# An attention kernel whose first batch scores both heads of a pair in turn, and whose batch-closing pairs spread their reciprocals by TensorE

## The chip, the cores and the metric

One Trainium2 chip, one of its cores. The metric is device time of the whole program in microseconds (us). Of the kernel before there are three runs with a median of 806.53 us (805.07 to 807.45).

## What is computed

Block-causal attention over 4 batches, 8 heads, 576 positions and a head size of 64, then a gated spatial unit, then a two-layer MLP with a residual. Cut to what matters here:

```python
scores = q @ k.T / sqrt(64)                 # per batch and head, 576 x 576
scores = where(row // 64 >= col // 64, scores, -1e9)
attn = exp(scores - max(scores))
attn = attn / (sum(attn) + 1e-9)
x = attn @ v                                # heads side by side: 576 x 512 per batch
h = relu(x @ w_in); u, v2 = split(h)        # 1024 columns
v_s = w_spatial @ layernorm(v2) + b_spatial
y = (u * v_s) @ w_out
out = y + relu(layernorm(y) * g @ w_ch1) @ w_ch2
```

## The kernel before

Attention goes by pairs of heads, four pairs to a batch, 16 in all. A pair is nine units (`UNITS`, line 231): first the last 64 rows of both heads together (chunk 4, two PSUM banks of 256 and 320 columns), then the chunks 3, 2, 1 and 0 of 128 rows, each for head 0 and then for head 1. The loop at line 533 runs over all units `u`. `scores(u)` (line 238) multiplies q and k into PSUM; `softmax(u)` (line 287) lets VectorE (DVE) mask the scores and take the minimum into an SBUF tile and ScalarE (ACT) take the exponential, with its sum into a column of `sm`; `transposes(u - 2)` (line 338) turns the result by TensorE into a PSUM bank, from which DVE or ACT copies it; `weighted` (line 389) multiplies it with v, in two parts (`pH` at the pair's unit 7, `pL` at unit 2 of the next pair), and ACT copies that out into `xx`.

The first `PACKED` = 4 pairs, which are batch 0, keep one head in the partitions 0 to 63 and the other in 64 to 127: a score product has 64 contraction rows, and a unit three products of split fp32 (high times high, high times low, low times high) into one bank. The first three units are plain fp32. From pair 4 on the splits are stacked to 128 rows and a unit has two products (line 281).

`reciprocals(p)` (line 310), at the first unit of the next pair, inverts the pair's row sums (128 partitions x 9 columns), transposes them, lets ACT copy them out, and spreads them over 64 partitions a head by a trip through DRAM: two stores, two loads that broadcast. `store_x(p)` (line 411), at unit 5 of the next pair, multiplies `xx` with them and splits the product into two fp32r parts in `xT`: three operations on GpSimd (POOL).

When a batch's four pairs are in `xT`, its products with `w_in` follow (`w_in_stage`, line 495: value tiles `vps`, then gate tiles `ups`). They are a generator from which `fill` (line 506) takes some products at each unit of the next batch, from the unit `dstart` = 8 of that batch on; the last batch's run after the loop. The weights `w_in` are unpacked (`decode`, line 81: ACT, then two operations on DVE, then two on POOL) at the units of the list `DECODE` (line 532), for the first time at unit 1.

PSUM has eight banks: three for matmul results (`p_mm`), three for scores (`p_sc`), two for transpositions (`p_tr`). Each engine works through its own queue in order. The order in the queues comes from the program's order and from a planner that simulates the program and moves ready instructions ahead. SP's queue issues all DMAs.

Of the kernel before, what the change touches and what calls it, by code (L numbers as in the profile page):

```python
# [8 lines left out]
F32 = mybir.dt.float32  # L9
# [4 lines left out]
ALU = mybir.AluOpType  # L14
AX = mybir.AxisListType
PSUM = bass.MemoryType.PSUM
# [17 lines left out]
def tile_kernel(  # L34
# [26 lines left out]
    NB, NP, _, _, _, S = qk.shape  # L61
# [7 lines left out]
    NPAIR = NB * NP  # L69
    MM = nc.tensor.matmul  # L70
# [66 lines left out]
    PACKED = PLAN['packed']  # L137
# [43 lines left out]
    idle = p_mm.tile([128, 512], F32, tag="mm", name="idle")  # L181

    def warm(n):
        for _ in range(n):
# [11 lines left out]
    ops = {}  # L196
# [35 lines left out]
    NU = len(UNITS)  # L232
    PLAIN = PLAN['plain']
    state = {}

    sums = {}

    def scores(u):
        p = u // NU
        j, c = UNITS[u % NU]  # L240
        st, qt, _, raw = ops[p]
        banks = []
        plain = u < PLAIN
        if c == 4:
            sums[p] = at.tile([128, 9], F32, tag="sm", name="sm")
            for a, z in ((0, 256), (256, S)):
                s_ps = p_sc.tile([128, 512], F32, tag="sc", name="sc")
                for h in range(2) if plain else ():
                    rows = slice(64 * h, 64 * h + 64)
                    MM(  # L250
                        s_ps[rows, :z - a], lhsT=raw[rows, 0, 0, 512:S], rhs=raw[rows, 0, 1, a:z],
                        start=True, stop=True,
                    )
                if not plain and p < PACKED:
                    for n, (x, y) in enumerate(((0, 0), (0, 1), (1, 0))):
                        MM(s_ps[:, :z - a], lhsT=qt[:, x, 0, :], rhs=st[:, y, 1, a:z], start=(n == 0), stop=(n == 2))
                elif not plain:
                    for h in range(2):
                        for i in range(2):
                            MM(  # L260
                                s_ps[:, :z - a], lhsT=qt[:, i, h, :], rhs=st[:, h, 2, a:z],
                                start=(h == 0 and i == 0), stop=(h == 1 and i == 1),
                            )
                banks.append((s_ps, a, z - a))
        else:
            n = 128 * (c + 1)
            nn = max(n, 192)
            q = slice(128 * c, 128 * c + 128)
            s_ps = p_sc.tile([128, 512], F32, tag="sc", name="sc")
            rows = slice(64 * j, 64 * j + 64) if j is not None else None  # L270
            if plain:
                MM(s_ps[:, :n], lhsT=raw[rows, 0, 0, q], rhs=raw[rows, 0, 1, 0:n], start=True, stop=True)
# [12 lines left out]
        state[u] = banks  # L285
# [20 lines left out]
        state[u] = (pt, n)  # L306

    rb_t = {}

    def reciprocals(p):  # L310

        sm = sums.pop(p)
        nc.vector.tensor_scalar(sm, sm, 1e-9, None, op0=ALU.add)
        nc.vector.reciprocal(sm, sm)
        ps = p_tr.tile([128, 512], F32, tag="tr", name="rps")
        nc.tensor.transpose(ps[:9, :128], sm, idn)
        rr = at.tile([128, 128], F32, tag="rr", name="rr", bufs=1)
        nc.scalar.copy(rr[:9], ps[:9, :128])
# [19 lines left out]
    def transposes(u):  # L338
# [8 lines left out]
                nc.scalar.copy(out, src)  # L347

        def flip(k0, k1):
            tr = p_tr.tile([128, 512], F32, tag="tr", name="tr")  # L350
# [38 lines left out]
    def weighted(p, part):  # L389
# [11 lines left out]
        ps = p_mm.tile([128, 512], F32, tag="mm", name="pv")  # L401
        for n, (kc, rows, a, z) in enumerate(jobs):
            for j in (1, 0):
                MM(  # L404
# [6 lines left out]
    def store_x(p):  # L411
        b, hp = divmod(p, NP)
        xx = xx_t.pop(p)
        E('xm', p).tensor_tensor(xx, xx, rb_t.pop(p), op=ALU.mult)
        c0 = (b % 2) * S
# [29 lines left out]
    def value_tile(pair, t):  # L445

        cols = slice(128 * t, 128 * t + 128)
        flush()
        ps = p_mm.tile([128, 512], F32, tag="mm", name="vps")
# [24 lines left out]
    def gate_unit(b, fc):  # L474
        c0 = (b % 2) * S
        ur = dn.tile([128, S], F32, tag="ur", name="ur")
        for h in range(2):
            cols = slice(c0 + HS * h, c0 + HS * h + HS)
            flush()
            ps = p_mm.tile([128, 512], F32, tag="mm", name="ups")  # L480
# [88 lines left out]
    at.release()  # L569
    p_tr.release()  # L570
    p_sc.release()


    sy = tc.alloc_tile_pool(name="sy", bufs=1, side="right", reuse_waits="tile")
# [84 lines left out]
        fetch_vn(n)  # L659
    dn.release()  # L660
    xw.release()
    p_mm.release()

    w1p = tc.alloc_tile_pool(name="w1p", bufs=1, side="left", reuse_waits="tile")
# [494 lines left out]
```

## Time and profile before

| | |
|---|---|
| median of three runs | 806.53 us |
| the profiled execution | 807.45 us, span 805.5 us |
| mean granted TensorE clock | 0.997 |
| TensorE (PE) busy | 781.1 us, 97% |
| VectorE (DVE) | 528.4 us, 66% |
| ScalarE (ACT) | 419.2 us, 52% |
| GpSimd (POOL) | 413.8 us, 51% |
| attention in pairs 0 to 3 | up to about 53 us |
| attention in pairs 4 to 15, with the products with w_in | to about 265 us |
| last products with w_in, spatial unit, MLP | the rest |

Line numbers are those of the code above. PE is TensorE's matmuls, PEld its weight loads, which overlap them. Matmuls are pipelined: one has a start, and an end that lies after the start of the next, so busy times of several overlap, and how long a run of them holds the engine is read from its start to the start of what follows. A group in a timeline shows the shape of its first matmul alone. A fp32 matmul appears as two instructions. The clock is the share that was granted of 2.4 GHz.

### The profile page before, as it was taken

To read this page: it belongs to the slowest core of one execution; us is meant where nothing else is said; L and a number is where in the kernel's file an instruction comes from. 1 tells how busy PE (TensorE), PEld (TensorE's weight loads), DVE (VectorE), ACT (ScalarE), POOL (GpSimd) and SP (SyncE) were. 2 spreads that over 40 slices of the span, in tenths; PEclk is the share of its full clock that TensorE was granted. 3 is DMA by queue.
4 is the path that set the end of the run, shared out by engine and by line. 5 is a ranking of instruction groups with operands and counts; after the bars stand their busy time and mean duration, and the time that the engine had idled before them with its cause. 6 is when DMAs were issued, how large, how long until landed. Compare 5 with 4: busy or idle time off the path is not lost.

```text
span 805.5 us, 13270 instructions
## 1 busy us (share of the span) xinstructions
PE 781.1 (97%) x4498; PEld 667.3 (83%) x4498; DVE 528.4 (66%) x1193; ACT 419.2 (52%) x1071; POOL 413.8 (51%) x417
## 2 busy tenths in 40 slices
PE   9998999999999999899999999999999999999997
PEld 4666788778878799888888888888899888888986
DVE  5777666674564377776677777897566578645534
ACT  5777676566755454555354554553345454433421
POOL 5598866654543343222275455455545455545431
PEclk9999999999999999999999999999999999999999
DMA  8966445545251579778520333204001003000002
GB/s 245 208 169 175 130 134 152 141 124 168 68 158 51 151 223 284 214 243 272 165 92 0 105 115 96 79 1 157 1 15 39 1 1 123 22 0 1 1 1 78
DMA packets 53687, 88.66 MB, mean 110 GB/s; under 512 B 6770, under 2 KB 17138, under 8 KB 53620
## 3 DMA queue, kind: packets, MB, share of 16 engines
q1 hardware_dynamic: 53620, 87.83, 36.7%
q8 instruction: 35, 0.57, 0.3%
q14 instruction: 32, 0.26, 0.1%
HBM read 68.85 MB, written 18.95 MB: 109 GB/s over the span
## 4 chain that ended last, share of the span: by engine, by line
PE 72%; DVE 11%; DMA 6%; issue 3%; ACT 3%; POOL 3%; SPq 0%; ACTq 0%; DVEq 0%; POOLq 0%
PE hps L938 21%; PE o L106 8%; PE o L108 8%; PE o L107 8%; PE pv L404 5%; PE tr L353 4%; DMA raw<-in_w_ch_dram 3%; PE sc L281 3%; PE ups L106 2%; PE sc L275 2%; DVE pH L345 2%; PE ups L108 2%; PE ups L107 2%; PE vps L108 1%; PE vps L106 1%
## 5 line engine op out<-in xcount | busy, mean ns | idle before, releaser
L102 POOL TENSOR_TENSOR a<-s,a 128x256 fp32r<-128x256 f32 x96 | 78.2, 818 | 92.4 <-ACT a L97 92.4
L107 PE MATMUL o<-w,h 128*128 128x512 f32 x288 | 112.9, 393 | 0.0
L106 PE MATMUL o<-w,h 128*128 128x512 f32 x288 | 107.8, 398 | 1.6 <-ACT h L930 1.6
L944 DVE TENSOR_TENSOR c<-hps,c 128x384 f32<-128x384 f32 x120 | 66.5, 554 | 54.1 <-PE hps L938 52.3
L108 PE MATMUL o<-w,h 128*128 128x512 f32 x288 | 97.7, 398 | 0.3
L303 ACT ACTIVATE p<-p,nm 128x512 f32<-128x512 f32 (+3 forms) x128 | 71.2, 557 | 34.1 <-DVE nm L296 31.0
L296 DVE CUSTOM_DVE_ANT_0 p<-sc,mask 128x512 f32<-128x512 f32 (+3 forms) x128 | 58.9, 479 | 41.7 <-PE sc L281 16.4
L102 POOL TENSOR_TENSOR a<-w,a 128x256 fp32r<-128x256 f32 x72 | 60.7, 846 | 44.9 <-ACT a L97 39.4
L97 ACT CAST a<-s 128x256 fp32r<-128x256 f32 x96 | 38.4, 404 | 83.6 <-PE hps L938 76.5
L345 DVE COPY pH<-tr 128x512 f32<-128x512 f32 (+1 forms) x88 | 49.7, 575 | 26.0 <-PE tr L353 25.3
L106 PEld LDWEIGHTS o<-w,h 128*128 128x128 f32 x288 | 53.7, 187 | 12.3 <-ACT h L930 2.9
L107 PEld LDWEIGHTS o<-w,h 128*128 128x128 f32 x288 | 54.1, 188 | 10.1
L108 PEld LDWEIGHTS o<-w,h 128*128 128x128 f32 x288 | 53.1, 188 | 9.3 <-DVE h L931 1.6
L353 PE MATMUL tr<-idn,p 128*128 128x128 f32 x320 | 56.1, 283 | 4.2 <-DVE pH L345 4.2
L788 POOL TENSOR_TENSOR gt<-gf,gt 128x576 fp32r<-128x576 f32 (+1 forms) x17 | 25.6, 1507 | 61.8 <-ACT gt L787 61.8
L117 POOL TENSOR_TENSOR rs<-rs,nhalf 128x1 f32<-128x1 f32 x36 | 23.0, 639 | 59.2 <-DVE rs L116 54.0
L353 PEld LDWEIGHTS tr<-idn,p 128*128 128x128 f32 x320 | 38.4, 142 | 14.8 <-DVE pH L345 6.7
L88 ACT ACTIVATE dm<-raw 128x256 f32<-128x256 f32 (+1 forms) x72 | 31.9, 462 | 29.9 <-DVE w L90 9.1
L221 POOL TENSOR_TENSOR stack<-qkt,stack 64x576 fp32r<-64x576 f32 x24 | 34.5, 1436 | 25.0 <-ACT stack L58 24.0
L931 DVE SCALAR_TENSOR_TENSOR h<-c,h 128x384 fp32r<-128x384 f32 x72 | 45.4, 650 | 1.5 <-ACT h L930 1.5
L281 PE MATMUL sc<-stack 128*128 128x512 f32 (+3 forms) x192 | 43.7, 341 | 0.8 <-DVE nm L296 0.4
L930 ACT ACTIVATE h<-c 128x384 fp32r<-128x384 f32 x72 | 35.3, 520 | 16.6 <-DVE c L944 16.2
(183 smaller groups left out, 2257.1 us busy)
## 6 DMA issues: line engine op xcount, KB each, us to landing
raw<-in_w_ch_dram SPq DMA_DIRECT2D x64, 256.0 KB
qkt<-in_qk_dram SPq DMA_DIRECT2D x112, 144.0 KB
vt<-in_v_dram SPq DMA_DIRECT2D x16, 320.0 KB
rb<-r_d SPq DMA_DIRECT2D x32, 144.0 KB
u_d<-ur SPq DMA_DIRECT2D x16, 288.0 KB
us<-u_d SPq DMA_DIRECT2D x16, 288.0 KB
y_d<-ys SPq DMA_DIRECT2D x18, 256.0 KB
yr<-y_d SPq DMA_DIRECT2D x18, 256.0 KB
```

The lines of the kernel that those rows point to most:

```text
L102: {"v": nc.vector, "g": nc.gpsimd}[low].tensor_tensor(lo, src, f32(hi), op=ALU.subtract)
L106: MM(out_ps, lhsT=a[0], rhs=b[0], start=first, stop=False)
L107: MM(out_ps, lhsT=a[0], rhs=b[1], start=False, stop=False)
L108: MM(out_ps, lhsT=a[1], rhs=b[0], start=False, stop=last)
L281: MM(s_ps[:, :nn], lhsT=st[:, j, i, q], rhs=st[:, j, 2, 0:nn], start=(i == 0), stop=(i == 1))
L296: nc.vector.tensor_tensor_reduce(pt[:, o:o + n], s_ps[:, :n], m, -0.125, 3e38, ALU.add, ALU.min, nm[:, i:i + 1])
L303: nc.scalar.activation(pt[:, :n], pt[:, :n], AF.Exp, bias=nm[:, 0:1], scale=-1.0, accum_out=sm[:, col:col + 1])
L345: nc.vector.tensor_copy(out, src)
L353: nc.tensor.transpose(tr[:, o:o + 128], pt[:, 128 * kc:128 * kc + 128], idn)
L931: nc.vector.scalar_tensor_tensor(t[:, 1], src, 0.0, f32(t[:, 0]), op0=ALU.max, op1=ALU.subtract)
L938: MM(ps, lhsT=a[x], rhs=b[y], start=not more and kc == 0 and k == 0, stop=kc == KD // 2 - 1 and k == 2, skip_group_check=True,)
L944: nc.vector.tensor_tensor(out, ps, x, op=ALU.add)
```

## The change

Three edits.

1. In pairs 0 to 3 the first head's unit of a chunk issues the products of both heads, head by head in turn, into a tile of two PSUM banks, one bank for each; the second head's unit issues none and its softmax reads the second bank. The chunk of 64 rows takes such a tile for its two banks.
2. While pairs 0 to 3 run, PSUM is laid out as two tiles of two banks for scores, three banks for transpositions and one for matmul results; from pair 4 on as before (three, two and three), the new banks lying where the released ones were.
3. The last pair of batch 0 (pair 3) and the last of all (pair 15) no longer send their reciprocals through DRAM: DVE copies the nine transposed rows, and ten TensorE products with a broadcast column of the identity spread them over the partitions in two PSUM banks. `store_x` for them comes two units earlier and runs on DVE alone. The products of batch 0 with `w_in` may begin at unit 6 of batch 1 instead of 8, and the last four decodes of `w_in` move from the units 38, 42, 46, 50 to 42, 45, 48, 51.

Its core:

```diff
-    p_mm = tc.alloc_tile_pool(name="p_mm", bufs=PLAN["mm"], space=PSUM, side="left")
-    p_sc = tc.alloc_tile_pool(name="p_sc", bufs=PLAN["sc"], space=PSUM, side="right")
-    p_tr = tc.alloc_tile_pool(name="p_tr", bufs=PLAN["tr"], space=PSUM, side="right")
+    p_mm = tc.alloc_tile_pool(name="p_mm", bufs=1, space=PSUM, side="left", reuse_waits="tile")
+    p_tr = tc.alloc_tile_pool(name="p_tr", bufs=2, space=PSUM, side="right", reuse_waits="tile")
+    p_tr3 = tc.alloc_tile_pool(name="p_tr3", bufs=1, space=PSUM, side="right", reuse_waits="tile")
+    p_two = tc.alloc_tile_pool(name="p_two", bufs=2, space=PSUM, side="right", reuse_waits="tile")
...
+    def mm_bank(name):                      # tr_bank likewise: p_tr, every third time p_tr3
+        turns[0] += 1
+        pool = single[1] if single and turns[0] % 3 else p_mm
+        return pool.tile([128, 512], F32, tag="mm", name=name)
...
+        if p < PACKED and j != 1:
+            two = p_two.tile([128, 2, 512], F32, tag="two", name="sc")
...
             elif p < PACKED:
-                for i, (x, y) in enumerate(((0, 0), (0, 1), (1, 0))):
-                    MM(
-                        s_ps[:, :nn], lhsT=st[rows, x, 0, q], rhs=st[rows, y, 1, 0:nn],
-                        start=(i == 0), stop=(i == 2),
-                    )
+                for i, (x, y) in enumerate(((0, 0), (0, 1), (1, 0)) if j == 0 else ()):
+                    for h, rows in enumerate(halves):
+                        MM(
+                            two[:, h, :nn], lhsT=st[rows, x, 0, q], rhs=st[rows, y, 1, 0:nn],
+                            start=(i == 0), stop=(i == 2),
+                        )
...
+    BY_MATMUL = (NP - 1, NPAIR - 1)
...
         nc.tensor.transpose(ps[:9, :128], sm, idn)
         rr = at.tile([128, 128], F32, tag="rr", name="rr", bufs=1)
+        if p in BY_MATMUL:
+            nc.vector.tensor_copy(rr[:9], ps[:9, :128])
+            ra = mm_bank("ra")
+            rt = tr_bank("rt")
+            for c in range(5):
+                for j in range(2):
+                    half = slice(64 * j, 64 * j + 64)
+                    row = 8 if c == 4 else 4 * j + c
+                    MM(
+                        rt[half, 0:64] if c == 4 else ra[half, 128 * c:128 * c + 128],
+                        lhsT=idn[0:9, row:row + 1].to_broadcast([9, 64]),
+                        rhs=rr[0:9, half] if c == 4 else rr[0:9], start=True, stop=True,
+                    )
+            rb_t[p] = (ra, rt)
+            return
...
+        if p in BY_MATMUL:                  # store_x
+            ra, rt = rb_t.pop(p)
+            nc.vector.tensor_tensor(xx[:, 0:512], xx[:, 0:512], ra, op=ALU.mult)
+            nc.vector.tensor_tensor(xx[:, 512:S], xx[:, 512:S], rt[:, 0:64], op=ALU.mult)
+            split(xx, *[x[:, hp, c0:c0 + S] for x in xT], "v", "v")
+            del ops[p]
+            return
...
-    DECODE = {1, 7, 12, 17, 22, 38, 42, 46, 50}
+    DECODE = {1, 7, 12, 17, 22, 42, 45, 48, 51}
...
+        if u == PACKED * NU:
+            p_two.release()
+            p_tr3.release()
+            single[:] = [
+                tc.alloc_tile_pool(name="p_sc", bufs=3, space=PSUM, side="right", reuse_waits="tile"),
+                tc.alloc_tile_pool(name="p_mm2", bufs=2, space=PSUM, side="left", reuse_waits="tile"),
+            ]
...
-        if i == D + 3 and 1 <= p <= NPAIR:
+        if 1 <= p <= NPAIR and i == (D + 1 if p - 1 in BY_MATMUL else D + 3):
             store_x(p - 1)
...
-            if k == PLAN['dstart'] and b <= NB - 1:
+            if k == (6 if b == 1 else PLAN['dstart']) and b <= NB - 1:
                 dense = chain(dense, w_in_stage(b - 1))
```

## Rows read from the trace of the kernel before

**Rows 1.** The page: the chain that ended last, by engine.

```profile
PE 72%; DVE 11%; DMA 6%; issue 3%; ACT 3%; POOL 3%; SPq 0%; ACTq 0%; DVEq 0%; POOLq 0%
```

**Rows 2.** Windows: length, busy us of PE, PEld, DVE, ACT, POOL; clock, DMA share, GB/s.

```profile
12.00:53.00 41.00, 38.07 (x270) 26.39 (x271) 30.74 (x99) 32.82 (x104) 29.11 (x29) 1.00 0.85 222
53.00:68.00 15.00, 12.22 (x87) 8.64 (x87) 9.34 (x30) 13.53 (x35) 14.02 (x11) 0.97 0.48 123
65.00:70.00 5.00, 3.92 (x21) 2.80 (x21) 3.40 (x4) 3.73 (x9) 4.42 (x5) 0.71 0.42 118
68.00:82.00 14.00, 13.18 (x85) 10.20 (x82) 11.86 (x34) 8.06 (x27) 11.59 (x11) 0.91 0.76 199
82.00:806.00 724.00, 706.81 (x4034) 618.37 (x4032) 471.92 (x1017) 361.27 (x901) 353.86 (x356) 1.00 0.33 100
58.35:74.02 15.67, 12.64 (x80) 9.04 (x79) 10.70 (x32) 11.78 (x33) 14.61 (x13) 0.89 0.56 165
126.47:140.37 13.90, 13.47 (x104) 11.14 (x103) 7.21 (x28) 10.37 (x31) 6.80 (x5) 1.00 0.56 145
```

**Rows 3.** The same window of pair 8, the gate tiles `ups` alone (PE, PEld, ACT).

```profile
126.47:140.37 13.90, 3.81 (x24) 3.29 (x24) 0.82 (x2) 1.00 0.56 145
```

**Rows 4.** TensorE's timeline: start, length, engine, line, group, count.

```profile
17.88 0.96 PE L275 MATMUL sc<-stack 64*128 64x512 f32 x3
...
19.14 0.96 PE L275 MATMUL sc<-stack 64*128 64x512 f32 x6
...
23.59 0.63 PE L275 MATMUL sc<-stack 64*128 64x256 f32 x6
...
26.68 0.87 PE L404 MATMUL pv<-pL,vt 128*64 128x256 f32 x8
...
38.16 0.60 PE L275 MATMUL sc<-stack 64*128 64x192 f32 x6
...
45.56 0.79 PE L275 MATMUL sc<-stack 64*128 64x384 f32 x3
...
67.05 1.55 PE L404 MATMUL pv<-pL,vt 128*64 128x256 f32 x8
```

**Rows 5.** Windows of pairs 1 to 3, line 275 alone (PE, PEld, clock, DMA).

```profile
15.00:28.50 13.50, 4.50 (x24) 2.71 (x24) 1.00 0.97 262
28.50:42.00 13.50, 4.28 (x24) 2.73 (x24) 1.00 0.93 216
42.00:52.03 10.03, 4.09 (x24) 2.55 (x24) 1.00 0.55 166
```

**Rows 6.** Waits from 12 to 68 us: who for whom, us, times, longest.

```profile
DVE pH L345 <- PE tr L353: 6.4, 7, 2.1
...
DVE p L296 <- PE sc L275: 4.7, 5, 1.9
...
PE tr L353 <- DVE pH L345: 1.5, 4, 0.4
```

**Rows 7.** DVE's groups over the span: busy us, mean ns, idle before.

```profile
L944 DVE TENSOR_TENSOR c<-hps,c 128x384 f32<-128x384 f32 x120 | 66.5, 554 | 54.1 <-PE hps L938 52.3
...
L610 DVE TENSOR_TENSOR ws<-wn,ws 128x576 fp32r<-128x576 f32 x4 | 3.4, 862 | 16.1 <-ACT ws L609 16.1
```

**Rows 8.** Chain that ended last, 57 to 82 us: start, length, what.

```profile
67.45 1.20 DVE de L89
...
68.77 1.68 DVE dm L90
...
79.11 1.41 POOL xT L417
```

**Rows 9.** TensorE's timeline at the last pair.

```profile
264.53 0.27 PE L316 MATMUL rps<-idn,sm 128*9 128x128 f32 x1
...
275.69 0.96 PE L108 MATMUL vps<-win,xT 128*128 128x512 f32 x3
...
276.88 0.50 PE L106 MATMUL vps<-win,xT 128*128 128x512 f32 x1 [0.22 <-ACT vr L459]
```

More of the change, by code (lines that the diff above doesn't have):

```diff
@@ L127, in tile_kernel, with tr_bank, sc_bank @@
     at = tc.alloc_tile_pool(name="at", bufs=2, side="right")
-    p_mm = tc.alloc_tile_pool(name="p_mm", bufs=PLAN["mm"], space=PSUM, side="left")
-    p_sc = tc.alloc_tile_pool(name="p_sc", bufs=PLAN["sc"], space=PSUM, side="right")
-    p_tr = tc.alloc_tile_pool(name="p_tr", bufs=PLAN["tr"], space=PSUM, side="right")
+    p_mm = tc.alloc_tile_pool(name="p_mm", bufs=1, space=PSUM, side="left", reuse_waits="tile")
+    p_tr = tc.alloc_tile_pool(name="p_tr", bufs=2, space=PSUM, side="right", reuse_waits="tile")
+    p_tr3 = tc.alloc_tile_pool(name="p_tr3", bufs=1, space=PSUM, side="right", reuse_waits="tile")
+    p_two = tc.alloc_tile_pool(name="p_two", bufs=2, space=PSUM, side="right", reuse_waits="tile")
+    single = []
+    turns = [0, 0]
+    def mm_bank(name):
+        turns[0] += 1
+        pool = single[1] if single and turns[0] % 3 else p_mm
+        return pool.tile([128, 512], F32, tag="mm", name=name)
+    def tr_bank(name):
+        turns[1] += 1
+        pool = p_tr if single or turns[1] % 3 else p_tr3
+        return pool.tile([128, 512], F32, tag="tr", name=name)
+    def sc_bank():
+        return single[0].tile([128, 512], F32, tag="sc", name="sc")
     win = [xw.tile([128, KD, 2 * F], F32R, name=f"win{i}") for i in range(2)]
@@ L180, in tile_kernel @@
     zeros = mask[:, 0:256].bitcast(BF16)
-    idle = p_mm.tile([128, 512], F32, tag="mm", name="idle")
+    idle = mm_bank("idle")
     def warm(n):
@@ L234, in tile_kernel @@
     state = {}
+    heads = {}
     sums = {}
@@ L246, in scores @@
             for a, z in ((0, 256), (256, S)):
-                s_ps = p_sc.tile([128, 512], F32, tag="sc", name="sc")
+                s_ps = two[:, a // 256] if p < PACKED else sc_bank()
                 for h in range(2) if plain else ():
@@ L268, in scores @@
             q = slice(128 * c, 128 * c + 128)
-            s_ps = p_sc.tile([128, 512], F32, tag="sc", name="sc")
-            rows = slice(64 * j, 64 * j + 64) if j is not None else None
-            if plain:
-                MM(s_ps[:, :n], lhsT=raw[rows, 0, 0, q], rhs=raw[rows, 0, 1, 0:n], start=True, stop=True)
-            elif p < PACKED:
-                for i, (x, y) in enumerate(((0, 0), (0, 1), (1, 0))):
-                    MM(
-                        s_ps[:, :nn], lhsT=st[rows, x, 0, q], rhs=st[rows, y, 1, 0:nn],
-                        start=(i == 0), stop=(i == 2),
-                    )
+            halves = (slice(0, 64), slice(64, 128))
+            if p >= PACKED:
+                s_ps = sc_bank()
+            elif j == 0:
+                heads[c] = two
+            if p < PACKED:
+                s_ps = heads[c][:, j]
+            if plain:
+                if j == 0:
+                    for h, rows in enumerate(halves):
+                        MM(
+                            two[:, h, :n], lhsT=raw[rows, 0, 0, q], rhs=raw[rows, 0, 1, 0:n], start=True, stop=True,
+                        )
+            elif p < PACKED:
+                for i, (x, y) in enumerate(((0, 0), (0, 1), (1, 0)) if j == 0 else ()):
+                    for h, rows in enumerate(halves):
+                        MM(
+                            two[:, h, :nn], lhsT=st[rows, x, 0, q], rhs=st[rows, y, 1, 0:nn],
+                            start=(i == 0), stop=(i == 2),
+                        )
             else:
@@ L314, in reciprocals @@
         nc.vector.reciprocal(sm, sm)
-        ps = p_tr.tile([128, 512], F32, tag="tr", name="rps")
+        ps = tr_bank("rps")
         nc.tensor.transpose(ps[:9, :128], sm, idn)
         rr = at.tile([128, 128], F32, tag="rr", name="rr", bufs=1)
+        if p in BY_MATMUL:
[6 more added lines that the diff above has]
+                    row = 8 if c == 4 else 4 * j + c
+                    MM(
+                        rt[half, 0:64] if c == 4 else ra[half, 128 * c:128 * c + 128],
+                        lhsT=idn[0:9, row:row + 1].to_broadcast([9, 64]),
+                        rhs=rr[0:9, half] if c == 4 else rr[0:9], start=True, stop=True,
+                    )
+            rb_t[p] = (ra, rt)
+            return
         nc.scalar.copy(rr[:9], ps[:9, :128])
@@ L349, in flip @@
         def flip(k0, k1):
-            tr = p_tr.tile([128, 512], F32, tag="tr", name="tr")
+            tr = tr_bank("tr")
             for kc in range(k0, k1):
@@ L400, in weighted @@
         src = pT_of(p)[part]
-        ps = p_mm.tile([128, 512], F32, tag="mm", name="pv")
+        ps = mm_bank("pv")
         for n, (kc, rows, a, z) in enumerate(jobs):
@@ L413, in store_x @@
         xx = xx_t.pop(p)
+        c0 = (b % 2) * S
+        if p in BY_MATMUL:
[5 more added lines that the diff above has]
+            return
         E('xm', p).tensor_tensor(xx, xx, rb_t.pop(p), op=ALU.mult)
-        c0 = (b % 2) * S
         cp('xh', p, xT[0][:, hp, c0:c0 + S], xx)
@@ L448, in value_tile @@
         flush()
-        ps = p_mm.tile([128, 512], F32, tag="mm", name="vps")
+        ps = mm_bank("vps")
         for kc in range(KD):
@@ L479, in gate_unit @@
             flush()
-            ps = p_mm.tile([128, 512], F32, tag="mm", name="ups")
+            ps = mm_bank("ups")
             for kc in range(KD):
@@ L569, in tile_kernel @@
     at.release()
+    single[0].release()
     p_tr.release()
-    p_sc.release()
     sy = tc.alloc_tile_pool(name="sy", bufs=1, side="right", reuse_waits="tile")
@@ L661, in tile_kernel @@
     xw.release()
+    single[1].release()
     p_mm.release()
```

## The prediction

> **What bounds the kernel now.** I read the page first: TensorE is busy for 97% of the span, and nearly three quarters of the chain that ended last is on it [rows 1]. That is a mean over stages, so I next split the span into windows [rows 2]. From 82 us on TensorE is busy 706.8 of 724 us: whatever is gained earlier, the rest follows it. The change lies before that, apart from the last pair at 264 us. There two stretches differ. From 12 to 53 us (pairs 0 to 3, scores with 64 contraction rows) TensorE is busy 38.1 of 41 us, ACT 32.8, DVE 30.7. From 53 to 68 us TensorE is busy only 12.2 of 15 us, while ACT has 13.5 and POOL 14.0; and from 65 to 70 us the granted clock is 0.71, so part of that ran at 1.2 GHz, behind TensorE's idling. The first stretch is TensorE's, with two engines not far behind; in the second TensorE is starved.
>
> Then TensorE's timeline. Its lengths run to the last matmul's end, so a run of one has the same tail as a run of six, and the two can be compared. The three score products of one head, 512 columns each, take 0.96 us (17.88). From 19.14 six products take 0.96 us too: three of one head and three of the other [rows 4]. Where the order of instructions happened to mix the heads, which sit in different halves of the array's rows, the second head is free already in this trace.
>
> **The scores in turn (edit 1).** The windows of line 275 add up what pairs 1, 2 and 3 pay for 24 products each: 4.50, 4.28 and 4.09 us, 12.87 together [rows 5]. With both heads always in turn a pair has four runs of six: chunk 3 at 0.96, chunk 2 at the 0.79 of one head's three (45.56), chunk 1 at 0.63 (the six of 23.59), chunk 0 at 0.60 (the six of 38.16), together 2.98 [rows 4], for three pairs 8.94. Saved: 3.9 us. Pair 0 I cost at nothing: its scores lie between first loads, fixed filler products and first softmax; ends 0 and another third of 3.9, 1.3 us.
>
> How much comes through? 3.9 us off 41 leaves 37.1, with ACT's 32.8 and DVE's 30.7 in them: 88% and 83%. They can follow, though not without waits, since scores and exponentials feed each other. From 12 to 68 us DVE's copies wait 6.4 us for TensorE's transpositions and its minima 4.7 us for the scores of line 275, while TensorE's transpositions wait 1.5 us for DVE [rows 6]: mostly DVE follows TensorE. I take three quarters, 2.9 us, nearer to what these rows say than to nothing; ends 0 and 3.9.
>
> **The banks (edit 2).** A third transposition bank while pairs 0 to 3 run takes off some of the four waits of TensorE's transpositions for DVE's copies (1.5 us [rows 6]). I take 0.5; ends 0 and the 2.9 us that TensorE idles from 12 to 53. One matmul bank instead of three: a pair has two weighted sums, and the copy that frees the bank is of 256 or 320 columns, less than the 0.55 us that DVE takes for 384 [rows 7], against some 13 us a pair; nothing, and one such copy for each of eight sums, 4.4 us, if ACT never came in time. Scores in two tiles of two banks give a bank back only after both heads' minima, one minimum later than now (again under 0.55 us). A whole chunk is scored ahead, so I cost it at nothing, at most 4 x 0.55 = 2.2 us if the look-ahead runs dry once a pair. At pair 4 the single banks come out of these tiles, and its first scores wait for pair 3's last minimum once: inside edit 3's lower end.
>
> **The end of the first batch (edit 3).** Two windows run from the first weighted sum of a pair to that of the next: up to pair 4's (58.35 to 74.02, 15.67 us) and up to pair 8's (126.47 to 140.37, 13.90 us) [rows 2]. Both have 128-row scores, but pair 8 holds 24 products with w_in, busy 3.8 us [rows 3], and pair 4 none. So pair 8's own work fits in some 10 us and pair 4 loses 5 or more. To what? POOL is busy 14.6 of the 15.7 us (pair 8: 6.8 of 13.9) and ACT 11.8 [rows 2], and the chain of waits goes through DVE's decode of one w_in tile, 1.20 and 1.68 us, and last through a POOL operation of 1.41 us, x's low part, for which the value products wait [rows 8]. Part is clock: the eight products of the weighted sum at 67.05 take 1.55 us, at 26.68 0.87 [rows 4].
>
> What goes: the decode of unit 38 moves to 42, the others back by 3, 2 and 1. The reciprocals' trip through DRAM and POOL's three operations go; x's low part, now done at 80.52 [rows 8], no longer stands in POOL's queue behind decodes. Two stores and two loads a pair leave SP's queue, and the loads of later pairs behind them go out earlier; no wait of TensorE for a load stands in the windows above, so I count nothing. What comes: on DVE a copy of nine rows, the products with x out of PSUM (0.554 us for 384 columns gives 0.74 for 512, and 0.2 for 64), a cast and a subtraction (0.86 for 576 [rows 7], and I take half of it for the cast): 2.3 us. On TensorE twenty fp32 instructions, 1152 columns for each half of the array's columns: the eight of 26.68 have 768 for each half and take 0.87 us [rows 4], so 1.3 us if the halves run side by side as there, 2.6 if not. At pair 3 they fall into the stall. While they stand, one of two transposition banks is held until x is made, and transpositions go one bank at a time. The value products may begin at unit 42, and the same work is missing later, before unit 80, where pair 8 shows little waiting. I take 2.0 us of the 5, as DVE gets x while ACT keeps its load; ends +5 and -6 (rival 3).
>
> **The last pair (edit 3 again).** Here TensorE isn't starved. From the transposition of the sums at 264.53 it runs on w_in products that need no x of pair 15, and it waits only at 275.69, where three products with a length of 0.96 us stand before the next start at 276.88 [rows 9]: at most 0.5 us of waiting. The new products cost 1.3 us there. Net I take -0.6 (some of them beside other waits); ends +0.5 and -2.1 (not side by side).
>
> **Sum**: 2.9 + 0.5 + 2.0 - 0.6 = 4.8 us. The profiled execution took 807.45 us (span 805.5, 1.95 around it), so 802.65 on its scale; that run is 0.92 above the median of 806.53 to which the result is compared: 801.7.
>
> **Rivals.** 0.3% is 2.4 us, about what a measurement of this kernel can tell from no change.
> 1. The forecast: most of the scores' saving comes through and part of the stall goes. 798 to 804. Chance 0.55.
> 2. ACT and DVE take over the pace of pairs 0 to 3. For: ACT at 88% of the shortened stretch, with an exponential behind each minimum. Against: DVE's waits above. Then scores and banks give 1, edit 3 gives 1, less 0.6: 1.4 gained, 805.1. Chance 0.17. The Trainium skill, "TensorEngine Tiling (Array Packing)", section Performance Considerations, warns of this: packing speeds up TensorE but not the emptying of PSUM, which may become the bottleneck. The windows show the emptying engines at 75% and 80% before the change, so the rule doesn't bite yet; by it edit 1 would give nothing.
> 3. Slower: DVE is overloaded from unit 39 to 51. x adds 2.3 us, and three decodes stand three units apart beside the value tiles' normalization, when one has taken 2.9 us. DVE is busy 11.9 of 14 us from 68 to 82 [rows 2]; 2.3 more is 14.2. It decides if each of the four late decodes holds a minimum up by 1.5 us with the transpositions on one bank: -6 on edit 3, +2.9, +0.5 and -0.6 elsewhere, 3.2 lost: 809.7. Against: POOL, in whose company the slow decode ran, loses three operations. Chance 0.13.
> 4. All of the stall goes, and the clock with it: 3.9 + 1.5 + 5 - 0.6 = 9.8 gained, 796.7. Chance 0.15.
> That the heads don't run side by side is excluded by the six in 0.96 us.
>
> **How the numbers follow.** Faster is 1 and 4, 0.70; the same is 2, 0.17; slower is 3, 0.13. Predicted is the first rival's middle, 801.7. The range runs from 796.0, just under rival 4's time, over the rivals 1 and 2 to 807.5; it leaves out most of rival 3 and what lies under rival 4 (0.06), together 2 in 10.
>
> **What would show it.** Right: score runs of six with 0.96, 0.79, 0.63 and 0.60 us in TensorE's timeline; pair 3's first weighted sum, now at 58.35, 3 us earlier; no stretch near 65 us with the clock at 0.71; x of pair 3 done before 75. Edit 3 is wrong if transpositions wait for DVE at pair 4, or if the window from there to pair 4's stays at 15 us without w_in products in it. At the last pair there should be a run of 1.3 us and no gap at 275. The forecast is wrong if pair 3's first weighted sum comes no earlier than 57, or if TensorE idles more from 53 us on than now.

## The result: slower, by one helper of the change

| | median (range), runs | ratio to before [95%] |
|---|---|---|
| before | 805.78 us (804.22 to 807.45), 6 | 1 |
| after | 813.62 us (808.36 to 817.33), 6 | 1.0082 [1.0055, 1.0110] |
| after, one result pool instead of two (E17) | 803.35 us (801.54 to 807.31), 8 | 0.9949 [0.9924, 0.9973] |

I had said faster, 801.7 us; the change is 0.8% slower. The third row is the same change with one thing undone, found at the end of the experiments: it is 0.5% faster than the kernel before by the runs beside it, whose median was 807.30 us. Against the median of all 147 runs of the kernel before, 805.63 us, it is 0.3% faster. In four of the twenty profiled executions (E7, E9, E15 and E18) pair 0's sum begins 4 to 5 us later than in kernels with the same code up to there (last section), so the leads below are read from the other sixteen, and a median can hold more or fewer such late starts.

### The profile after

The profiled execution took 817.33 us, span 815.5. The page, the chain that ended last by engine: where POOL had 3% [rows 1], it has 7%.

```profile
PE 71%; DVE 8%; POOL 7%; issue 5%; DMA 4%; ACT 4%; SPq 1%; ACTq 0%; POOLq 0%; DVEq 0%
```

Windows, columns as in [rows 2]: first from pair 2's weighted sum to pair 3's, then two of fixed length, then up to pair 8's sum.

```profile
40.88:57.93 17.05, 12.44 (x79) 8.46 (x77) 8.18 (x27) 11.08 (x34) 16.49 (x16) 0.80 0.58 151
...
50.00:60.00 10.00, 8.39 (x50) 5.84 (x50) 3.01 (x12) 7.17 (x22) 9.63 (x10) 0.67 0.57 161
...
138.00:146.00 8.00, 6.62 (x32) 5.25 (x33) 3.62 (x12) 3.73 (x12) 5.59 (x4) 0.57 0.28 82
...
131.65:147.54 15.89, 13.47 (x79) 10.11 (x79) 9.02 (x33) 9.88 (x29) 7.05 (x6) 0.79 0.48 128
```

Up to pair 3's sum POOL works 16.49 of 17.05 us, and the granted clock is 0.80 on the mean; up to pair 8's sum it is 0.79, where [rows 2] had 1.00 and 13.90 us with 24 gate products.

TensorE's timeline shows the scores as the change wants them, and the place where the first gain ends.

```profile
28.87 0.96 PE L304 MATMUL sc<-stack 64*128 64x512 f32 x6
32.33 1.15 PE L304 MATMUL sc<-stack 64*128 64x384 f32 x12
36.58 0.58 PE L304 MATMUL sc<-stack 64*128 64x192 f32 x6
...
51.02 0.48 PE L398 MATMUL tr<-idn,p 128*128 128x128 f32 x1 [4.03 <-ACT pL L392]
```

Pair 2's 24 score products now take 0.96 + 1.15 + 0.58 = 2.69 us (4.28 in [rows 5]); pair 1's take 3.03 (4.50). The sums of pairs 0, 1 and 2 begin at 17.79, 29.76 and 40.88 us, which is 2.2, 3.5 and 5.4 us earlier than in the kernel before. The first and the third of them, after and before:

```profile
17.79 2.27 PE L449 MATMUL pv<-pH,vt 128*64 128x320 f32 x20
...
40.88 0.75 PE L449 MATMUL pv<-pH,vt 128*64 128x320 f32 x2
```

```profile
20.03 2.27 PE L404 MATMUL pv<-pH,vt 128*64 128x320 f32 x20
...
46.27 2.28 PE L404 MATMUL pv<-pH,vt 128*64 128x320 f32 x20
```

Then TensorE stands 4.03 us for ACT's copies, and pair 3's sum begins at 57.93 (before: 58.35). ACT's and POOL's timelines tell why:

```profile
45.06 0.19 ACT L332 ACTIVATION_READ_ACCUMULATOR p<-p,nm 128x1 f32 x1
48.77 0.41 ACT L241 CAST qtail<-stack 128x256 fp32r<-128x256 f32 x1 [3.52 <-POOL stack L237]
```

```profile
34.94 1.42 POOL L467 TENSOR_TENSOR xx<-xx,rb 128x576 f32<-128x576 f32 x1 [5.55 <-DMA rb<-r_d]
...
44.39 1.40 POOL L237 TENSOR_TENSOR stack<-qkt,stack 64x576 fp32r<-64x576 f32 x1
45.87 1.41 POOL L239 TENSOR_TENSOR stack<-qkt,stack 64x576 fp32r<-64x576 f32 x1
47.35 1.39 POOL L237 TENSOR_TENSOR stack<-qkt,stack 64x576 fp32r<-64x576 f32 x1
```

The same operation of POOL in the kernel before:

```profile
32.75 1.42 POOL L414 TENSOR_TENSOR xx<-xx,rb 128x576 f32<-128x576 f32 x1 [1.24 <-DMA rb<-r_d]
```

In ACT's queue a copy of pair 4's operand (line 241) stands ahead of the exponentials of pair 3 and waits 3.52 us for POOL. POOL is late because it stood 5.55 us for the reciprocals of pair 0 (before: 1.24): TensorE had transposed them 2.5 us earlier than before, and they came through DRAM 2.2 us later (34.94 against 32.75). By then no products with w_in are ready to fill TensorE, and the clock goes to half.

The second loss is in the batches after it. The products with w_in, gate tiles up to the sums of pairs 6, 7 and 8, then value tiles up to pair 9's (columns of [rows 3]):

```profile
93.69:116.07 22.38, 9.66 (x57) 8.02 (x57) 1.13 (x3) 1.00 0.54 151
116.07:131.65 15.58, 6.67 (x39) 5.61 (x39) 2.02 (x5) 1.00 0.59 175
131.65:147.54 15.89, 0.00 (x0) 0.00 (x0) 0.00 (x0) 0.79 0.48 128
```

```profile
147.54:170.78 23.24, 12.07 (x48) 8.58 (x48) 2.38 (x4) 1.00 0.47 123
```

Batch 0's products are used up before the window of pair 8, which had 24 of them [rows 3]; TensorE runs dry there, and that is the second stretch at half clock.

The last pair, TensorE's timeline:

```profile
275.74 1.09 PE L356 MATMUL ra<-rr,idn 9*64 9x128 f32 x16 [0.37 <-DVE rr L349]
276.67 0.28 PE L356 MATMUL rt<-rr,idn 9*64 9x64 f32 x4
277.56 0.87 PE L449 MATMUL pv<-pL,vt 128*64 128x256 f32 x8 [0.36 <-ACT pL L392]
```

Twenty instructions, 0.93 us to the last four and 0.28 for these: the halves run side by side, as worked out from [rows 4].

### The profile page after: what moved, and what is told of

Read it like the earlier page. It is cut to its first block, busy times and chain, and to the rows that moved or that the text cites. A ratio compares the mean times of both kernels' runs of the same rounds, so it can differ in the third digit from the quotient of the medians.

```text
span 815.5 us, 13342 instructions
## 1 busy us (share of the span) xinstructions
PE 785.2 (96%) x4538; PEld 670.7 (82%) x4538; DVE 534.3 (66%) x1203; ACT 421.5 (52%) x1069; POOL 405.1 (50%) x411
## 4 chain that ended last, share of the span: by engine, by line
PE 71%; DVE 8%; POOL 7%; issue 5%; DMA 4%; ACT 4%; SPq 1%; ACTq 0%; POOLq 0%; DVEq 0%
PE hps L998 20%; PE o L106 8%; PE o L108 8%; PE o L107 7%; PE pv L449 4%; PE tr L398 3%; PE sc L310 2%; PE ups L106 2%; PE ups L108 2%; PE ups L107 2%; POOL stack L237 2%; POOL stack L239 2%; PE vps L106 1%; PE vps L107 1%; PE vps L108 1%
## 5 line engine op out<-in xcount | busy, mean ns | idle before, releaser
L390 DVE COPY pH<-tr 128x512 f32<-128x512 f32 (+2 forms) x88 | 50.2, 576 | 38.3 <-PE tr L398 38.0
L117 POOL TENSOR_TENSOR rs<-rs,nhalf 128x1 f32<-128x1 f32 x36 | 22.5, 624 | 67.8 <-DVE rs L116 67.3
```

Source lines behind the costliest of these rows:

```text
L390: nc.vector.tensor_copy(out, src)
```

## The experiments

Eighteen kernels, five rounds each, against runs of the kernel before made beside them. "Lead" is how much earlier than in the kernel before something begins, corrected where one of the two has done more w_in products by then (0.228 us for a value product, 0.133 for a gate product: their spacing in the timeline).

| | kernel | median us | ratio [95%] |
|---|---|---|---|
| E1 | after, products from unit 8 | 810.31 | 1.0076 [1.0047, 1.0105] |
| E2 | E1, old decodes | 810.47 | 1.0058 [1.0033, 1.0082] |
| E3 | edits 1 and 2 alone | 821.30 | 1.0189 [1.0152, 1.0226] |
| E4 | edit 3 alone | 806.05 | 1.0014 [0.9991, 1.0038] |
| E5 | E1, pair 4's copy on POOL | 809.02 | 1.0050 [1.0021, 1.0079] |
| E6 | E1, x of pair 0 late | 810.36 | 1.0042 [1.0018, 1.0066] |
| E7 | E1, one result pool | 809.40 | 1.0022 [0.9996, 1.0049] |
| E8 | E6 and E7 | 807.24 | 1.0005 [0.9985, 1.0026] |
| E9 | E5 and E7 | 807.47 | 1.0016 [0.9989, 1.0043] |
| E10 | E3, one result pool | 805.95 | 1.0014 [0.9988, 1.0040] |
| E11 | E10 and E5 | 806.78 | 1.0020 [0.9993, 1.0046] |
| E12 | E9, copies of pairs 4 to 6 on POOL | 804.97 | 0.9995 [0.9976, 1.0015] |
| E13 | E12, pair 4's operands half on DVE | 807.16 | 1.0025 [0.9998, 1.0052] |
| E14 | E12, pairs 4 and 5 | 807.94 | 1.0039 [1.0017, 1.0062] |
| E15 | before, relieved as E13 | 807.33 | 1.0031 [1.0009, 1.0053] |
| E16 | before, split result pool alone | 821.42 | 1.0183 [1.0152, 1.0213] |
| E17 | after, one result pool | 803.35 | 0.9949 [0.9924, 0.9973] |
| E18 | E12 without edit 3 at pair 3 | 805.52 | 0.9985 [0.9960, 1.0010] |

### First round: which edit

**E1**, batch 0's products start where they did:

```diff
-            if k == (6 if b == 1 else PLAN['dstart']) and b <= NB - 1:
+            if k == PLAN['dstart'] and b <= NB - 1:
```

> The changed kernel with one number back: batch 0's products with w_in may begin at unit 8 of batch 1 again, not 6. Theory T (the gain of the scores is given back in two places where TensorE has no other work: at 47 us, where ACT stands behind POOL's operands of pair 4, and before pair 8, because batch 0's products have run out): the window up to pair 8's first weighted sum gets products back and shrinks from 15.9 us less its products to about 11; 2 to 4 us less than the changed kernel, 810 to 811.5. The idle 4 us at 47 stay. Rival R (DVE is overloaded from unit 39 to 51 by x and by decodes three units apart): no difference, 813 to 814.

Pair 8's window has 12 gate products again and the full clock, and the median is 3.3 us lower; but the ratios differ by 0.06% with intervals over each other, so the times don't show it.

**E2**, E1 and the old decodes:

```diff
-    DECODE = {1, 7, 12, 17, 22, 42, 45, 48, 51}
+    DECODE = {1, 7, 12, 17, 22, 38, 42, 46, 50}
```

> As e1_start8, and the decodes of w_in back at units 38, 42, 46 and 50. T: the idle 4 us at 47 stay, the window up to pair 5's sum loses the 2.8 us that it has over the kernel before; 808 to 810. R: DVE gets room, 6 us less than the changed kernel, 806 to 808, with the difference in the windows of pairs 4 and 5 alone.

Not better in the median. R, my own third rival, loses its decodes: without the three close ones the kernel is as slow. Its other part, x of pair 3 on DVE, is still in E2; E4 tells of that.

**E3**, E2 without edit 3:

```diff
-    BY_MATMUL = (NP - 1, NPAIR - 1)
+    BY_MATMUL = ()
```

> The changed kernel without edit 3: reciprocals of all pairs by DRAM, x on POOL, old start and old decodes; scores in turn and the bank layout stay. T: pair 3's window still holds an idle stretch of TensorE near 47 us, since POOL's work up to there is the same; 805 to 808, that is the kernel before to 2 us above it. R: the scores' gain comes through, 801 to 803. A third theory, S (two tiles of two banks starve the softmax): score runs wait for minima in pairs 0 to 3 and the sums there come no earlier than before; 808 or more.

15 us slower than before: far outside the ranges of T and R. It lies in that of S (808 or more), but the sums of pairs 0 to 2 are 2.6, 3.9 and 5.7 us earlier, and S had them no earlier than before. So none of the three explains it.

**E4**, the kernel before with edit 3 and nothing else:

```diff
+    BY_MATMUL = (NP - 1, NPAIR - 1)
...
+            ra, rt = rb_t.pop(p)
...
+    DECODE = {1, 7, 12, 17, 22, 42, 45, 48, 51}
```

> The kernel before with edit 3 alone (reciprocals of pairs 3 and 15 by TensorE, x on DVE, start at unit 6, late decodes). T: no idle stretch at 47 us; value products begin some us before 76; the window up to pair 8's sum has few products and is longer than the 13.9 us of before less 3.8; 804 to 807. R: all of the loss is here, 810 or more.

No change, as T has it; R expected 810 or more here and falls. So edits 1 and 2 hold the loss, and not in the pairs they are made for.

### Second round: where edits 1 and 2 lose it

**E5**, E1 with one copy on another engine:

```diff
-        nc.scalar.copy(
+        (nc.gpsimd.tensor_scalar if p == PACKED else lambda o, i, *_, **k: nc.scalar.copy(o, i))(
             view(qt, 0, [[192, 2], [256, 2], [1, 64]]), f32(view(st, 512, [[3 * S, 2], [S, 2], [1, 64]])),
+            1.0, 0.0, op0=ALU.mult, op1=ALU.add,
         )
```

> The kernel after with batch 0's products starting at unit 8 again (810.3 us so far), and the last operand copy of pair 4 (line 241) on POOL instead of ACT. Three theories. M (memory): the faster pairs 0 to 2 only bring pair 0's reciprocals 3 us earlier into a stretch in which the loads hold the DMA queues, so they land no earlier (33.9 against 32.7 us), POOL stands 4.9 us before x of pair 0, all that stands behind it in POOL's queue is late, ACT stands in order behind pair 4's operand copy, and TensorE, with no other work, idles 3 us near 47 and then runs at half clock. V (volume): POOL simply has too much work from pair 2 to pair 4, whatever the order. B (banks): from batch 1 on the split result pool (one bank and two) costs 2 us and more. M expects ACT's wait near 45 us to be gone and TensorE's idling there down from 3.2 to under 1.5 us, but pair 4's first scores now wait for POOL itself: 806.5 to 809. V and B expect 810 to 811.

The median is level with the upper end of M's range. The stall is gone: the window up to pair 3's sum, and a later one.

```profile
40.41:52.90 12.49, 10.32 (x78) 6.70 (x77) 7.69 (x26) 10.59 (x33) 12.03 (x13) 1.00 0.54 151
76.00:84.00 8.00, 6.97 (x26) 5.01 (x26) 3.35 (x8) 5.74 (x14) 6.07 (x5) 0.57 0.73 171
```

12.49 us with the clock at 1.00, where E1 has 14.75 at 0.88 and the kernel after 17.05 at 0.80: ACT's wait behind POOL made that stall. But the lead of 5.5 us at pair 3's sum is 0.7 at pair 5's, with the half clock moved to 76 us.

**E6**, E1 with POOL's x of pair 0 behind the decodes (it landed behind pair 4's operands, too):

```diff
+        if p == 2 and i == D + 3:
+            store_x(0)
-        if 1 <= p <= NPAIR and i == (D + 1 if p - 1 in BY_MATMUL else D + 3):
+        if 2 <= p <= NPAIR and i == (D + 1 if p - 1 in BY_MATMUL else D + 3):
...
+        if p == 0:
+            tc.keep_in_program_order(ins)
```

> The kernel after with batch 0's products starting at unit 8 again, and POOL's x of pair 0 put behind the two decodes and behind pair 4's operands in POOL's queue, so that nothing stands behind the reciprocals of pair 0 while they are on their way. M expects POOL's 4.9 us of waiting before 34 us to be nearly gone, pair 4's operands some 4 us earlier, TensorE's idling in pair 3's window down from 3.2 to under 1.5 us and no half clock there: 804 to 807. V expects the same amount of POOL work to be late somewhere else, at x of pairs 0 to 2: 809 to 812. B expects 810 to 811.

POOL's waits from 29 to 60 us (who for whom, us, times, longest):

```profile
POOL xx L467 <- DMA rb<-r_d: 2.4, 1, 2.4
POOL stack L233 <- PE sc L304: 2.3, 1, 2.3
```

The wait is halved, pair 4's operands start at 39.0 us instead of 43.0 and the clock is 1.00 up to pair 3's sum, yet that sum begins at 60.5 us (E1: 56.0) and the median is that of E1. M names the chain rightly and not what the time hangs on.

**E7**, E1 with the result banks from pair 4 on in one pool:

```diff
-        pool = single[1] if single and turns[0] % 3 else p_mm
+        pool = single[1] if single else p_mm
...
+            p_mm.release()
...
-                tc.alloc_tile_pool(name="p_mm2", bufs=2, space=PSUM, side="left", reuse_waits="tile"),
+                tc.alloc_tile_pool(name="p_mm2", bufs=3, space=PSUM, side="left", reuse_waits="tile"),
```

> The kernel after with batch 0's products starting at unit 8 again, and from pair 4 on one pool of three result banks as in the kernel before, instead of one bank and two in a fixed turn. B expects the window after pair 12's sum back from 23.2 us with 48 value products to 18.7 with 36, TensorE's other work in each batch down by a microsecond: 807 to 809. M and V expect nothing from it: 810 to 811.

36 value products after pair 12's sum, as B expected; the median lies between the ranges of B and of M and V, and by the ratio it is nearer to before than E1, the intervals touching.

**E8**, both edits:

> The two edits before together. M and B together expect 801.5 to 805, faster than the kernel before; M alone 804 to 807; V alone 809 to 812.

Level with before; just above the range of M alone, and not the 801.5 to 805 of two causes that add.

### Third round: the pool, with and without the rest

**E9**, the edits of E5 and E7:

> Batch 0's products at unit 8, pair 4's last operand copy on POOL, and one pool of three result banks from pair 4 on: the edits of the two kernels that had them alone, together. If the wait of ACT behind POOL (worth some 1.3 to 2 us in the kernel with that edit alone) and the order that follows from the split pool (1 to 4 us) are two causes that add, 803.5 to 807, about the time of the kernel before; if they are the same microseconds, 808 to 810.

Just above the range for causes that add, and not apart from E7.

**E10**, E3 with E7's one pool:

> Edits 1 and 2 alone (reciprocals all through DRAM, products and decodes at their old units), with one pool of three result banks from pair 4 on; with the split pool this kernel took 821.3 us. B: the 15 us that were lost there came from the order that the split pool brings, most of it at the last batch, and go with it: 806 to 809. If the two-bank score tiles or the DRAM trip of the last pair were the cause, it stays at 815 to 821.

The two differ by the pool alone: 821.30 and 805.95 us, 15 us. B holds.

**E11**, E10 and E5's copy:

> The kernel before this one with pair 4's last operand copy on POOL. M and B: ACT's wait near 47 us is gone as well, 803 to 807; faster than the kernel with all three edits and these two if edit 3 costs as much as it cost alone (0.1%).

Within the range, no gain over E10.

**E12**, E9 with the copies of three pairs on POOL:

```diff
-        (nc.gpsimd.tensor_scalar if p == PACKED else
+        (nc.gpsimd.tensor_scalar if p < PACKED + 3 else
```

> All three edits, products at unit 8, one pool of three result banks, and the last operand copy of pairs 4, 5 and 6 on POOL, so that ACT waits for POOL at none of them. If ACT's order behind POOL is what costs TensorE its work and its clock near 47, 60 and 77 us, no half clock from 40 to 90 us and 801 to 805. If POOL's volume sets the pace there, its queue is 0.7 us a pair longer and the time 806 to 810.

Time as expected, level with before; the clock isn't: between the sums of pairs 4 and 5 its mean is 0.93.

### Fourth round: POOL's volume, and the pool alone

**E13**, E12 with half of pair 4's subtractions on DVE:

```diff
-            nc.gpsimd.tensor_tensor(st[high, j, 2, :], raw[high, j, 1, :],
+            (nc.vector if p < PACKED + 1 else nc.gpsimd).tensor_tensor(st[high, j, 2, :], raw[high, j, 1, :],
```

> The kernel with all three edits, one result pool and the last operand copies on POOL (805.0 us), and two of the four subtractions that make pair 4's operands (line 239) on DVE instead of POOL: 2.9 us less for POOL before pair 4, two operations of under 0.9 us more for DVE. V (POOL's volume from 40 to 60 us takes edit 1's gain): 800 to 803.5, pair 3's and pair 4's sums earlier by 1 to 2 us. If DVE or something else takes the gain: 804 to 807.

**E14**, the same with `PACKED + 2`:

> The same for pairs 4 and 5: 5.8 us less for POOL up to 70 us. V: 798.5 to 802.5. If DVE, which is busy for 94% from 60 to 70 us, is the next bound: 804 to 807.

**E15**, the kernel before with E12's copies and E13's line:

> The kernel before with the same relief as in the first of this call (pair 4's two subtractions on DVE, the last operand copies of pairs 4 to 6 on POOL), nothing of the change. If POOL sets the pace from 40 to 60 us in the kernel before too (busy 14.6 of 15.7 us in the window of pair 4), the relief alone gives 2 to 4 us: 801.5 to 804, and edit 1 adds little to it. If POOL matters only once edit 1 has pulled the pairs forward: 804.5 to 806.

All three medians are above E12's and before's, and the intervals of E14 and E15 lie above 1. V isn't borne out: POOL's relief gains nothing, with the change or without it. But it loads DVE, where one of the moved subtractions took from 0.76 us (E13) to 1.92 (E15), so what POOL's volume costs by itself isn't shown.

**E16**, the kernel before with its result pool split, and nothing of the change:

```diff
-    p_mm = tc.alloc_tile_pool(name="p_mm", bufs=PLAN["mm"], space=PSUM, side="left")
+    p_mm = tc.alloc_tile_pool(name="p_mm", bufs=1, space=PSUM, side="left")
+    p_mm2 = tc.alloc_tile_pool(name="p_mm2", bufs=2, space=PSUM, side="left")
+    turns = [0]
+
+    def mm_bank(name):
+        turns[0] += 1
+        return (p_mm2 if turns[0] % 3 else p_mm).tile([128, 512], F32, tag="mm", name=name)
```

> The kernel before with its three result banks split into one and two in a fixed turn, nothing else of the change. B (the split pool costs time by itself from batch 1 on): 808 to 815, the pattern of value products after pair 12's sum 48 instead of 36. If it does so only together with the two-bank tiles: 805 to 806.

This run settles that the pool is the cause: 15 us (1.83%) with the same eight banks, the same work and the sums of pairs 0 to 4 as before to 0.1 us. It is more than the 808 to 815 that B expected, and the pattern is not quite B's: 39 value products after pair 12's sum, not 48. What differs is the order of TensorE's queue. The value products from pair 4's sum to its last weighted sum, in the kernel before and in E16:

```profile
74.02:82.47 8.45, 3.56 (x12) 2.03 (x12) 0.58 (x1) 1.00 0.68 143
```

```profile
74.08:84.29 10.21, 6.24 (x24) 4.21 (x24) 0.60 (x1) 1.00 0.57 118
```

Where one value tile (12 products) stood ahead of the weighted sum, two stand ahead of it. At pair 8 it is the same: between its first and its last weighted sum stand 12 value products in the kernel before, 27 in E16 and 35 in the kernel after. With one pool the sum asked for its tile earlier than the second value tile and was served first; a tile whose turn falls on the other pool can overtake. That is my reading of the code; the trace shows the overtaking. So w_in products go early, and are missing at a batch's end. E16's gate products in the windows up to the sums of pairs 11 and 12, and TensorE's timeline after pair 15's sum:

```profile
182.77:204.60 21.83, 11.69 (x75) 10.41 (x75) 2.83 (x7) 1.00 0.55 167
204.60:215.43 10.83, 0.00 (x0) 0.00 (x0) 0.00 (x0) 1.00 0.23 68
```

```profile
285.83 0.79 PE L106 MATMUL vps<-win,xT 128*128 128x512 f32 x1 [5.11 <-POOL xT L60]
```

75 products in one window, none in the next, and at the end nothing to cover the reciprocals' trip through DRAM: 5.11 us idle. E3 has the same counts there, and the same loss. Of the 12.2 us between the two profiled spans (817.7 and 805.5), 7.7 are more idling of TensorE, whose busy time is 785.6 and 781.1 us; why it is busy 4.5 us longer isn't shown. Waiting for a result bank of the right pool is little of it: TensorE's waits for ACT to copy a result out before a w_in product are 1.5 us in E16 and 0.5 in the kernel before.

### Fifth round

**E17**, the change with E7's diff alone, its products from unit 6:

> The kernel after with one pool of three result banks from pair 4 on in place of one bank and two in a fixed turn; all else as in the change, products from unit 6 too. If the split pool is what makes the change slower: 805 to 809, the same as the kernel before within 0.4%, with 36 value products after pair 12's sum. If the early start of the products or the decodes cost as much: 810 to 813.

Faster than all I expected. Its window up to pair 8's sum, a stretch in it, its gate products there, and the value products after it:

```profile
126.39:140.09 13.70, 13.35 (x103) 11.21 (x103) 7.14 (x27) 10.33 (x31) 7.56 (x6) 1.00 0.51 151
...
138.00:146.00 8.00, 8.00 (x54) 6.09 (x53) 5.91 (x20) 4.90 (x15) 7.57 (x6) 1.00 0.49 143
```

```profile
126.39:140.09 13.70, 3.78 (x24) 3.29 (x24) 0.82 (x2) 1.00 0.51 151
```

```profile
140.09:159.02 18.93, 9.51 (x36) 6.40 (x36) 1.76 (x3) 1.00 0.54 143
```

24 gate products and 36 value products, the counts of before, and the clock stays up. The stall near 47 us is in it too, as long as in E1 (2.26 us):

```profile
49.48 0.33 PE L398 MATMUL tr<-idn,p 128*128 128x128 f32 x1 [2.26 <-ACT pL L392]
```

So that stall is not what makes the change slower than before; the pool is.

Against E7, which differs by the start at unit 8 alone (1.0022), the intervals don't meet, but E7's profiled execution began late (last section), so the medians may not compare like with like. What the traces show of the start at unit 6 is the last window above, from pair 8's sum to pair 9's: 18.93 us here and 18.92 in E4, the other kernel with one pool and that start, against 20.29 to 20.31 in the kernel before and all ten with one pool and the start at unit 8, with 36 value products in each. That is 1.4 us.

**E18**, E12 with the old decodes and edit 3 for the last pair alone:

```diff
-    BY_MATMUL = (NP - 1, NPAIR - 1)
+    BY_MATMUL = (NPAIR - 1,)
```

> One result pool, both heads in turn, three transposition banks, reciprocals by TensorE for the last pair alone, products and decodes at their old units, and the last operand copies of pairs 4 to 6 on POOL. If edit 3 costs at pair 3 what the kernel with edit 3 alone showed there (near 3 us up to pair 9) and gives something at the last pair: 802 to 804.5, faster than before. If edit 1's gain is lost by pair 5 whatever stands there: 804.5 to 807.

Level with before, as the second reading has it: leaving out edit 3 at pair 3 gains nothing.

## Why the prediction was wrong

**The step that failed** is the banks (edit 2). I put "one matmul bank instead of three" at nothing for pairs 0 to 3, and costed no result bank from pair 4 on, where three stand again. What stands ahead of the prediction calls them "as before", and that was wrong: three there are, but in two pools with a fixed turn, and that let w_in products overtake weighted sums in the later batches: 14.7 us in the kernel before (E16, 0.0183 x 805), 15 in edits 1 and 2 (E3 to E10), and 10.3 between the medians of after and E17. I counted banks and not who may have which. My own window of pair 8, with its 24 products [rows 3], was the row that could have warned: what fills a later stretch is set by an order.

**The scores** gave more than I forecast: 3.03 us in pair 1 and 2.69 in pair 2 where I had 2.98 for each, and the lead at pair 2's sum is 5.4 us. 2.2 of it are there at pair 0's sum, which I put at nothing, and 1.2 and 1.9 come at the next two, together what their products save (1.5 and 1.6) and not three quarters of it. No run has edit 1 without edit 2, so what part is the third transposition bank's, put at 0.5, isn't shown.

**"They can follow"**: until pair 2, ACT and DVE do, and the rule that I weighed there (the Trainium skill, "TensorEngine Tiling (Array Packing)", section Performance Considerations), that the emptying of PSUM may become the bottleneck, doesn't bite in this trace up to there. But the lead meets POOL, which I read in [rows 2] as 14.6 of 15.7 us busy and didn't weigh, and ACT's in-order wait behind it.

**The end of the first batch**: 2.0 us forecast, and lost instead. In E17, where the pool is undone, the lead is 5.2 us at pair 2's sum, 1.6 at pair 3's, 0.3 at pair 8's, 1.7 at pair 9's, 2.6 at the MLP's first product and 3.9 at the end (spans of 801.6 and 805.5). So that stretch costs 4.9 us, and later stretches give some back; 1.3 us of that come in the MLP, which the change doesn't touch. Nor is it edit 3 that takes the lead: in E10, which hasn't got it, the lead goes from 5.5 to 0.3 between the same two sums. My test for it, pair 3's sum no later than 57, failed at 57.93, and the low clock at 65 us went only to come at 50.

**The last pair**: 0.93 and 0.28 us, 1.2 where I said 1.3; what edit 3 nets there, put at -0.6, isn't shown. **Rival 3** had the sign and not the cause (E2 and E4).

With the pool undone the total has the sign of the 4.8 us forecast: 0.51% of 805.8 is 4.1 us (2.2 to 6.1) by the runs beside E17, and 2.3 us against all runs of the kernel before. That isn't the forecast proved: its terms were off on both sides, and that they come near in sum is luck.

**Open**: what takes the lead between pairs 3 and 5 where ACT's wait is gone (E5, E12) or POOL has less to do (E13, E14). In E12, whose lead falls from 4.6 us at pair 4's sum to 1.3 at pair 5's, the trace names DVE's queue: TensorE stands 2.22 us for a DVE copy, which stands behind statistics that wait for ACT, and from 88.1 us the clock is at half for 3.4 us.

```profile
88.31 0.88 PE L399 MATMUL tr<-idn,p 128*128 128x128 f32 x3 [2.22 <-DVE pH L391]
```

```profile
86.88 0.69 DVE L112 BATCH_NORM_STATS2 st<-vr 128x6 f32<-128x512 f32 x1 [1.73 <-ACT vr L512]
87.49 0.67 DVE L391 COPY pH<-tr 128x512 f32<-128x512 f32 x1
```

No run takes that wait away. Open too is how the start at unit 6 saves its 1.4 us with one pool, and why it shows nothing with two (E1). An order of the queue written out by hand, which would tell, wasn't tried.

## What to carry to other kernels

Where a planner orders the queues, the pool that a tile comes from is part of the order: two pools in a fixed turn are not one pool with as many buffers, and the cost can come hundreds of microseconds later. After such an edit compare the count of filler products window by window. And a lead in one stage is worth what the next in-order queue lets through: ask which engine is over 90% busy there, and what stands behind its next wait.

## What the hardware showed that I had not expected

A DVE operation on nine columns (the row sums, line 343) takes from 154 to 1418 ns. The timelines of DVE and POOL:

```profile
18.18 1.35 DVE L343 TENSOR_SCALAR sm<-sm 128x9 f32<-128x9 f32 x1
```

```profile
16.71 2.79 POOL L225 TENSOR_TENSOR stack<-qkt,stack 128x576 fp32r<-128x576 f32 x2 [2.48 <-ACT pH L392]
```

It began while POOL's second subtraction ran and ended 0.03 us after that, at 19.53. In the kernel before the same operation at 57.1 us took 1312 ns, ending 0.03 us after a POOL subtraction too; with POOL doing nothing at 32.5 us it took 160. The Trainium skill, "SBUF — State Buffer", section "SBUF: two separate sides", says that DVE and GpSimd share a port pair, which the first of a GpSimd operation and a DVE operation in a two-port mode or with two SBUF inputs holds for its whole instruction. The trace agrees with such a lock; it doesn't show in which mode the DVE operation was. It is one way in which POOL's 96% from 40 to 60 us can reach DVE, and it may be why E13 to E15 gained nothing; no run here took it away.

Reciprocals that were ready 2.8 us earlier (ACT's copy at 21.92 against 24.71 us) came through DRAM 2.2 us later, with the DMA share at 0.85 from 12 to 53 us in both kernels. SP issued the first store 1.8 us after the copy (before: at once), and the loads 4.8 us after it had issued the second store (before: 2.4). That the bulk loads in the queues made the difference is my reading; no run moved them.

TensorE's first products differ from one execution to the next. E17 and E7 are the same code up to pair 4, and so are these two:

```profile
6.09 1.12 PE L298 MATMUL sc<-qkt 64*128 64x512 f32 x2
```

```profile
6.18 2.07 PE L298 MATMUL sc<-qkt 64*128 64x512 f32 x2
```

In E7, E9 and E18 the products are so long up to 16 us, in E15 up to 13.5, and pair 0's sum begins at 22.5 to 23.8 us, against 17.0 to 20.1 in the other sixteen profiled executions. The lengths are as at half clock (1.55 and 0.87 us in [rows 4]), although the clock's column has 1.00 for these windows. It is worth 4 to 5 us, as much as the whole lead of pairs 0 to 2, and nothing in these kernels was changed for it.
